# The last 128 rows of a matmul kernel in three column pieces (256, 128, 128) instead of two (256, 256)

## The chip, the cores and the metric

One core of one Trainium2 chip. The metric is the device time of one execution in microseconds; runs of one kernel mostly agree within 0.3%, and the trace of one profiled execution goes with each run. For the stretch that is changed I also use a finer measure, called the *tail*: from the start of the first matmul of the last 128 rows to the end of the span, both read from the trace. The tail leaves out the scatter of the 295 us ahead of it.

Some runs come out longer at a lower granted TensorE clock (0.983 to 0.987 here, where the others have 0.993 to 1.0). A run counts as slow when it is over 1.5% above the fastest of its kernel; ratios use the other runs, called fast.

## The reference

Attention over keys and values that are averaged in groups of 8, then a gated feed-forward layer. Only the last line matters here: the last matrix product.

```python
attn = softmax(scale * q @ pooled_k.T) @ pooled_v     # B=8, H=8, S=576, D=64
x = attn.transpose(0, 2, 1, 3).reshape(4608, 512)
h = x @ w_in                                          # 512 -> 2048
g = h * np.cos(h)
out = (g @ w_out).astype(np.float32)                  # 2048 -> 512
```

## The kernel before

Tokens are taken in 9 blocks of 512. For each, 2048 features are computed ("up", L297), gated (cos on ScalarE, product on VectorE), and multiplied back to 512 columns ("down", L310) in four chunks of 128 rows, `ms` = 0 to 3. Each chunk sums 16 matmuls in one PSUM bank. VectorE copies the bank to a buffer `o_sb` (L316), and two DMAs write 64 rows each to memory (L320). The very last chunk is done by `last_chunk`, which already cuts the 512 columns in two, so that the first half is copied and sent while the second is computed.

```python
msb = ctx.enter_context(tc.tile_pool(name="msb", bufs=3))     # o_sb, below, has 3 buffers
# ... (cut)
def down_out(t, ms, ps, c0=0, queues=(nc.sync, nc.sync)):
    o = msb.tile([128, d_model], FP32, name="o_sb", tag="o_sb")
    n = ps.shape[1]
    nc.vector.tensor_copy(out=o[:, 0:n], in_=ps)
    rows_of = out.rearrange("(b p t) m -> b t p m", b=B, t=ROW)
    for i, rows in enumerate(half):
        b_, pos = divmod((t * TILE + ms * 128) // 64 + i, ROW)
        queues[i].dma_start(out=rows_of[b_, ORDER[pos], :, c0:c0 + n], in_=o[rows, 0:n])

def last_chunk():
    t, ms = NT - 1, 3
    for hc in range(2):
        ps = banks[hc][:, 0, 0:256]
        for fc in range(FFCH):                                # FFCH = 16
            nc.tensor.matmul(ps, lhsT=g_sb[:, fc, ms * 128:(ms + 1) * 128],
                             rhs=w_out_sb[fc // 4][:, fc % 4, hc * 256:(hc + 1) * 256],
                             start=(fc == 0), stop=(fc == FFCH - 1))
        down_out(t, ms, ps, hc * 256, (nc.sync, nc.scalar))
# ... (cut)
        for n, (ms, fc) in enumerate(mms):                    # the other chunks
            # ... (cut)
            down_mm(obanks[ms % 2], ms, fc)
            if fc == FFCH - 1:
                down_out(t, ms, obanks[ms % 2])
    # ... (cut)
    last_chunk()
```

Every call of `down_out` takes the next of the three `o_sb` buffers, whatever the width of the piece. A copy into a buffer must wait until the two DMAs that last read that buffer have landed.

The softmax here doesn't subtract the row's maximum and nothing guards it: scores larger than these inputs give would overflow.

Of the kernel before, what the change touches and what calls it, by code (L numbers as in the profile page):

```python
# [19 lines left out]
def kernel(  # L20
# [9 lines left out]
    nc = tc.nc  # L30
# [31 lines left out]
    w_out_sb = [wpool.tile([128, 4, d_model], BF16, name=f"w_out_sb{i}") for i in range(4)]  # L62
# [9 lines left out]
    banks = [psum.tile([128, 2, 512], FP32, name=f"bank{i}") for i in range(3)]  # L72
# [240 lines left out]
# [9 lines that stand above are left out]
    def last_chunk():  # L322

        t, ms = NT - 1, 3
        for hc in range(2):
            ps = banks[hc][:, 0, 0:256]
            for fc in range(FFCH):
                nc.tensor.matmul(ps, lhsT=g_sb[:, fc, ms * 128:(ms + 1) * 128],  # L328
                                 rhs=w_out_sb[fc // 4][:, fc % 4, hc * 256:(hc + 1) * 256],
                                 start=(fc == 0), stop=(fc == FFCH - 1))  # L330
            down_out(t, ms, ps, hc * 256, (nc.sync, nc.scalar))


    EX = 5
# [90 lines left out]
    for t in range(NT):  # L425
# [69 lines left out]
        if b + 1 < B:  # L495
# [3 lines left out]
            pool_add(b + 1, "k")  # L499
            pool_add(b + 1, "v")  # L500
    last_chunk()
# [1 line left out]
_INS = ['q', 'k', 'v', 'moe_w_in', 'moe_w_out']  # L503
# [26 lines left out]
```

## Time and profile before

| | value | from |
|---|---|---|
| time | 305.36 us, median of 3 (304.97 to 305.43) | the runs |
| span of the profiled run | 303.0 us, clock 0.998 | the trace |
| first matmul of the last chunk | 295.56 us | timeline |
| end of its last matmul | 299.22 us | timeline: 295.56 + 3.66 |
| start and end of the last copy | 299.26, 299.68 us | timeline |
| last DMA issue, last landing | 299.71, 301.90 us | the trace's records of DMAs |
| tail | 302.96 - 295.56 = 7.40 us | the trace |

In the lines of the profile, PE is TensorE's matmuls, PEld its weight loads, DVE VectorE, ACT ScalarE and SP SyncE; a q, as in SPq, marks work of the engine's instruction queue, such as issuing a DMA. A DMA *lands* when its semaphore reports that its bytes are written. An entry such as L328 names the line of the kernel, `out<-in` the tiles, `x32` the count; a bracket holds the idle time before and what ended it. The durations of the copies, from the view of line L316 within the last 7 us (minimum / median / maximum in ns):

```profile
L316 DVE COPY o_sb<-bank x2: 425/426/426, 297.5 to 299.3; 128x256 f32<-128x256 f32 x2
L316 DVE COPY o_sb<-obank x1: 693/693/693, 295.8 to 295.8; 128x512 f32<-128x512 f32 x1
```

These two rows give the cost model of a copy that the prediction uses: 256 more columns cost 267 ns. The other lines that carry the argument stand in the prediction.

### The profile page before, as it was taken

To read this page: it belongs to the slowest core of one execution; us is meant where nothing else is said; L and a number is where in the kernel's file an instruction comes from. 1 tells how busy PE (TensorE), PEld (TensorE's weight loads), DVE (VectorE), ACT (ScalarE), POOL (GpSimd) and SP (SyncE) were. 2 spreads that over 40 slices of the span, in tenths; PEclk is the share of its full clock that TensorE was granted. 3 is DMA by queue.
4 is the path that set the end of the run, shared out by engine and by line. 5 is a ranking of instruction groups with operands and counts; after the bars stand their busy time and mean duration, and the time that the engine had idled before them with its cause. 6 is when DMAs were issued, how large, how long until landed. Compare 5 with 4: busy or idle time off the path is not lost.

```text
span 303.0 us, 4567 instructions
## 1 busy us (share of the span) xinstructions
PE 292.3 (96%) x1766; PEld 141.8 (47%) x1798; DVE 172.8 (57%) x211; ACT 206.8 (68%) x255; POOL 129.8 (43%) x92
## 2 busy tenths in 40 slices
PE   6899999999999999999999999999999999999995
PEld 2545544444544444444444544454444544444444
DVE  6458646564656465736575566656574657425712
ACT  3887896469866986698668876788569856605500
POOL 8553008975963893369534972399000000000000
PEclk9999999999999999999999999999999999999999
DMA  7999999739476935693369426952800330031032
GB/s 144 203 207 206 208 204 195 161 55 172 94 167 88 151 70 129 101 163 82 80 117 165 96 65 126 162 107 54 151 0 2 70 69 0 22 84 35 0 71 71
DMA packets 44006, 32.92 MB, mean 109 GB/s; under 512 B 22096, under 2 KB 39248, under 8 KB 43984
## 3 DMA queue, kind: packets, MB, share of 16 engines
q0 software_dynamic: 19744, 18.07, 38.4%
q1 hardware_dynamic: 24080, 14.42, 20.8%
q8 instruction: 14, 0.23, 0.3%
q10 hardware_dynamic: 160, 0.13, 0.2%
q14 instruction: 8, 0.07, 0.1%
HBM read 36.70 MB, written 9.44 MB: 152 GB/s over the span
## 4 chain that ended last, share of the span: by engine, by line
PE 88%; ACT 5%; issue 2%; DMA 2%; DVE 1%; DVEq 0%; ACTq 0%; POOLq 0%
PE bank L297 41%; PE obank L310 35%; PE bank L241 5%; PE bank L211 3%; DMA q_b<-in_q_dram 2%; ACT lnc L247 2%; ACT ex L218 1%; PE bank L328 1%; DVE xT L252 1%; ACT inv L248 1%; PE obank L157 0%; ACT L285 0%; PE obank L192 0%; ACT cos L304 0%; PE bank L165 0%
## 5 line engine op out<-in xcount | busy, mean ns | idle before, releaser
L310 PE MATMUL obank<-w_out_sb,g_sb 128*128 128x512 bf16 x542 | 130.5, 380 | 0.9
L297 PE MATMUL bank<-xT,w_in_sb 128*128 128x512 bf16 x563 | 125.7, 379 | 1.3
L304 ACT ACTIVATE cos<-bank,half_pi 128x1024 f32<-128x1024 f32 x72 | 80.0, 1113 | 62.2 <-PE bank L297 62.2
L307 DVE TENSOR_TENSOR g_sb<-bank,cos 128x1024 bf16<-128x1024 f32 x72 | 88.1, 1225 | 51.7 <-ACT cos L304 51.7
L297 PEld LDWEIGHTS <-w_in_sb 128*128 128x128 bf16 x576 | 56.1, 98 | 69.0 <-issue 2.8
L310 PEld LDWEIGHTS <-g_sb 128*128 128x128 bf16 x560 | 52.3, 98 | 57.0 <-issue 3.1
L252 DVE TENSOR_TENSOR xT<-bank,inv 64x512 bf16<-64x512 f32 (+1 forms) x72 | 45.3, 629 | 46.7 <-ACT inv L248 45.2
L141 POOL TENSOR_TENSOR kv_st<-kv_st 72x2048 f32<-72x2048 bf16 x12 | 48.7, 4062 | 35.0 <-DMA kv_st<-in_k_dram 35.0
L247 ACT ACTIVATE lnc<-bank 64x512 f32<-64x512 f32 (+1 forms) x72 | 39.2, 544 | 6.6 <-PE bank L241 5.6
L218 ACT ACTIVATE ex<-bank 72x1024 bf16<-72x1024 f32 (+1 forms) x40 | 35.5, 926 | 3.3 <-PE bank L211 3.2
L316 DVE COPY o_sb<-obank 128x512 f32<-128x512 f32 x35 | 24.2, 692 | 17.0 <-PE obank L310 13.4
L142 POOL TENSOR_TENSOR kv_st<-kv_st 72x1024 f32<-72x1024 f32 x12 | 28.2, 2348 | 1.0
L248 ACT ACTIVATE inv<-lnc 128x512 f32<-128x512 f32 (+1 forms) x36 | 21.0, 583 | 1.1
L241 PE MATMUL bank<-ex,vz 72*128 72x256 bf16 (+1 forms) x176 | 20.0, 243 | 0.2 <-ACT ex L218 0.2
L241 PEld LDWEIGHTS <-vz 72*128 72x128 bf16 x176 | 13.6, 97 | 10.2 <-DVE xT L252 1.7
L145 POOL TENSOR_TENSOR kp<-kv_st 72x512 bf16<-72x512 f32 x12 | 15.0, 1268 | 0.5
L211 PE MATMUL bank<-qT,kk 64*72 64x256 bf16 (+1 forms) x192 | 13.6, 252 | 0.9 <-ACT qT L193 0.5
L211 PEld LDWEIGHTS <-kk 64*72 64x72 bf16 x192 | 7.5, 109 | 11.1 <-issue 9.8
L285 ACT ACT_TABLE_LOAD x9 | 11.5, 1283 | 0.9 <-PEq L514 0.7
L288 ACT ACT_TABLE_LOAD x9 | 11.5, 1283 | 0.2
L494 POOL COPY gate<-kk 1x1 bf16<-1x1 bf16 x5 | 0.9, 179 | 24.1 <-DMA kk<-kp 24.1
L84 POOL DMA_DIRECT2D q_b<-in_q_dram x10 | 7.7, 772 | 2.8 <-DMA w_in_sb<-in_moe_w_in_dram 1.4
(55 smaller groups left out, 88.2 us busy)
## 6 DMA issues: line engine op xcount, KB each, us to landing
out_dram<-o_sb SPq DMA_DIRECT2D x70, 128.0 KB, 2.3
kv_st<-in_v_dram POOLq DMA_DIRECT2D x8, 576.0 KB, 13.3
kv_st<-in_k_dram POOLq DMA_DIRECT2D x7, 576.0 KB, 7.9
q_b<-in_q_dram POOLq DMA_DIRECT2D x6, 576.0 KB, 10.2
w_in_sb<-in_moe_w_in_dram POOLq DMA_DIRECT2D x4, 512.0 KB, 13.3
w_out_sb<-in_moe_w_out_dram POOLq DMA_DIRECT2D x4, 512.0 KB, 18.4
q_b<-in_q_dram POOLq DMA_DIRECT2D x4, 288.0 KB, 11.9
g_sb<-in_k_dram SPq DMA_DIRECT2D x1, 576.0 KB, 3.6
```

The lines of the kernel that those rows point to most:

```text
L141: add(out=s, in0=x[:, :, 0:4, :], in1=x[:, :, 4:8, :], op=ADD)
L142: add(out=s[:, :, 0:2, :], in0=s[:, :, 0:2, :], in1=s[:, :, 2:4, :], op=ADD)
L211: nc.tensor.matmul(pair[:Sp, bank, c:c + n].rearrange("p (g n) -> p g n", n=64), lhsT=kk[b % 2][half[r], h0 + i, 0:Sp], rhs=att["qT", b][h ...
L218: nc.scalar.activation(out=ex[:, 0:nh * n].rearrange("p (a n) -> p a n", a=2), in_=pair[:Sp, :, 0:nh * n // 2], func=ACTF.Exp, scale=scale ...
L241: nc.tensor.matmul(pair[:, hp, (i // 2) * n:(i // 2 + 1) * n], lhsT=vz[b % 2][:, pj, 2 * hp:2 * hp + 2, :].rearrange("p a d -> p (a d)"), ...
L247: nc.scalar.activation(out=lnc[half[1 - hp]], in_=pair[half[1 - hp], hp, 0:w], func=ACTF.Ln)
L252: nc.vector.tensor_mul(out=x_out(b, u, half[hp]), in0=cols(pair[half[hp], hp, :], u), in1=cols(inv[half[1 - hp]], u))
L297: nc.tensor.matmul(h[:, j, :], lhsT=w_in_sb[fc // 4][:, ki, (fc % 4) * 128:(fc % 4 + 1) * 128], rhs=xT[:, ki, t * TILE:(t + 1) * TILE], st ...
L304: nc.scalar.activation(out=cos, in_=h, func=ACTF.Sin, bias=half_pi[:, :1])
L307: nc.vector.tensor_mul(out=g_sb[:, 2 * fp:2 * fp + 2, :], in0=h, in1=cos)
L310: nc.tensor.matmul(o, lhsT=g_sb[:, fc, ms * 128:(ms + 1) * 128], rhs=w_out_sb[fc // 4][:, fc % 4, :], start=(fc == 0), stop=(fc == FFCH - 1))
L316: nc.vector.tensor_copy(out=o[:, 0:n], in_=ps)
```

## The change

A narrower last piece needs a shorter copy and a smaller transfer after the last matmul, when nothing else is left to overlap with. The price is 16 more matmuls, each with its own weight load.

```diff
     def last_chunk():
 
         t, ms = NT - 1, 3
-        for hc in range(2):
-            ps = banks[hc][:, 0, 0:256]
+        for i, (c0, n) in enumerate(((0, 256), (256, 128), (384, 128))):
+            ps = banks[i][:, 0, 0:n]
             for fc in range(FFCH):
                 nc.tensor.matmul(ps, lhsT=g_sb[:, fc, ms * 128:(ms + 1) * 128],
-                                 rhs=w_out_sb[fc // 4][:, fc % 4, hc * 256:(hc + 1) * 256],
+                                 rhs=w_out_sb[fc // 4][:, fc % 4, c0:c0 + n],
                                  start=(fc == 0), stop=(fc == FFCH - 1))
-            down_out(t, ms, ps, hc * 256, (nc.sync, nc.scalar))
+            down_out(t, ms, ps, c0, (nc.sync, nc.scalar))
```

## The prediction

> **What bounds the kernel now.** First the page: TensorE is busy for almost the whole span.
>
> ```profile
> span 303.0 us, 4567 instructions
> PE 292.3 (96%) x1766; PEld 141.8 (47%) x1798; DVE 172.8 (57%) x211; ACT 206.8 (68%) x255; POOL 129.8 (43%) x92
> ```
>
> The change is confined to the last 128 rows, so only the last 8 us can move. Next, the chain that ended last, in order of time, from 285 us on:
>
> ```profile
> 289.52 6.21 PE obank L310 x28
> 295.73 3.51 PE bank L328 x32
> 299.23 0.02 issue
> 299.26 0.42 DVE o_sb L316
> ```
>
> L328 is the changed loop, L316 the copy out of PSUM. The reader is to see matmuls without a gap, then one copy; nothing waits for an earlier engine. The timeline of the same stretch (start, duration, engine) gives the raw numbers:
>
> ```profile
> 295.35 3.59 PEld L328 LDWEIGHTS <-g_sb 128*128 128x128 bf16 x32
> 295.56 3.66 PE L328 MATMUL bank<-w_out_sb,g_sb 128*128 128x256 bf16 x32
> 297.51 0.43 DVE L316 COPY o_sb<-bank 128x256 f32<-128x256 f32 x1 [1.05 <-PE bank L328]
> 299.26 0.42 DVE L316 COPY o_sb<-bank 128x256 f32<-128x256 f32 x1 [1.32 <-PE bank L328]
> ```
>
> One matmul of 256 columns is recorded as 273 ns, so 32 of them step by (3.66 - 0.273) / 31 = 109 ns. The copy ends at 299.68. The rest of the span is shown by busy time per stretch (stretch, length, PE, PEld, DVE, ACT, POOL, clock, DMA share, GB/s):
>
> ```profile
> 299.90:300.80 0.90, 0.00 (x0) 0.00 (x0) 0.00 (x0) 0.00 (x0) 0.00 (x0) 1.00 0.00 0
> 300.80:301.60 0.80, 0.00 (x0) 0.00 (x0) 0.00 (x0) 0.00 (x0) 0.00 (x0) 0.96 0.64 164
> 301.60:303.00 1.40, 0.00 (x0) 0.00 (x0) 0.00 (x0) 0.00 (x0) 0.00 (x0) 0.50 0.00 0
> ```
>
> After the copy nothing moves for 0.9 us, bytes move for under 0.8 us, then comes about 1.1 us of closing semaphores and drains behind the last landing. The issues of that last piece (both start at 299.71) land after
>
> ```profile
> out_dram<-o_sb SPq DMA_DIRECT2D x1, 64.0 KB, 1.9
> out_dram<-o_sb ACTq DMA_DIRECT2D x1, 64.0 KB, 2.2
> ```
>
> so the last bytes are down at about 299.71 + 2.2 = 301.9. Of the 3.8 us from the last matmul's end (299.22) to the span's end, what depends on the piece's width is 0.42 us of copy and some of the 0.8 us of transfer. That is all that the change can attack.
>
> **What the Trainium skill says.** (1) "TensorE: Matmul & The Clock Gate", section "Back-to-back issue gap": a sustained stream of weight load and matmul at N=128 costs about 81 ns per matmul, an isolated stream N/2.4 + 2.5, about 56 ns. The trace has 128-column matmuls with new weights each time, the q transposes:
>
> ```profile
> 31.30 0.67 PE L192 MATMUL obank<-identity,q_b 128*128 128x128 bf16 x9
> ```
>
> Each is recorded as 219 ns, so they step by (0.67 - 0.219) / 8 = 56 ns: the trace sides with 56, and I use 57. The 256-column step of 109 ns agrees with N/2.4 + 2.5. (2) "VectorE: DVE Perf Modes", section "Why PSUM operands drop a tier": fp32 out of PSUM goes at one element per cycle, 0.96 GHz. The trace agrees: 693 ns at 512 columns, 426 at 256 (rows of L316), 1.04 ns per column, 159 ns fixed. (3) "DMA: Bandwidth & Descriptors", section "Anatomy of one DMA — SWDGE (gpsimd) path": about 2 us of a DMA are fixed, mostly the receipt of the last write. That is the other issuing path, but the trace agrees in kind: 128 KB land in 2.2 to 2.4 us, 64 KB in 1.9 to 2.2. (4) The same page's "Specifications": rows from 512 B up keep line rate. A 128-column float32 row is exactly 512 B; no output of this trace has that size.
>
> **The change part by part.** The second piece of 256 columns becomes two of 128.
>
> *TensorE.* Removed 16 x 109 = 1.744 us, added 32 x 57 = 1.824 us: +0.08 us. Starting at 295.56, the first piece takes 1.744, so B starts at 297.30 and C at 298.22; the last matmul starts at 298.22 + 15 x 0.057 = 299.07 and ends at 299.29 instead of 299.22. On the path: +0.07. B's end is 297.30 + 15 x 0.057 + 0.219 = 298.38.
>
> *Copies.* Each 128-column copy takes 159 + 128 x 1.04 = 292 ns. B's runs 298.41 to 298.70, under C's matmuls, free. C's is on the path in place of 426 ns: -0.13.
>
> *The output buffer.* Here is a new wait. o_sb has three buffers, and each piece takes one, so C takes that of the third-last write, the 512-column chunk copied at 295.76. The instruction order of the changed kernel, built but not run, confirms it: its last copy waits for exactly the two DMAs of that chunk. Before, the last copy waited for the chunk of 292.31, long landed. The second half of that chunk was issued at
>
> ```profile
> 297.00 0.65 SPq L320 DMA_DIRECT2D out_dram<-o_sb  x1
> ```
>
> and the DMA row for this issue alone says
>
> ```profile
> out_dram<-o_sb SPq DMA_DIRECT2D x1, 128.0 KB, 2.4
> ```
>
> hence landed at about 299.4. C's matmuls are done at 299.29, so the copy would be held about 0.11 us, and with two or three semaphore waits of the DVE's queue (36 ns median) it starts at about 299.48 instead of 299.33. Price: +0.15 on the path. C's copy then ends at 299.48 + 0.29 = 299.77, against 299.68: so up to the copy the change loses 0.09 us.
>
> *DMA.* B's two issues start at 298.73. SP is free (A's issue 297.97 + 0.47) and so is ACT (297.97 + 0.53). They end near 299.25, before C needs the queues, and B's bytes land near 300.8, just before C's start moving at about 299.80 + 1.1 = 300.9. C's two DMAs carry 32 KB each instead of 64. From 128 to 64 KB the landing on SP fell by 0.3 to 0.5 us, so halving again saves perhaps half as much, 0.15 to 0.25 (an estimate from these two sizes). Last landing: 299.80 + 2.2 - 0.2 = 301.8, against 301.9. The closing 1.1 us stays, with perhaps two more already satisfied semaphore waits of 28 ns: +0.03.
>
> Sum: TensorE +0.07, copy -0.13, buffer wait +0.15, DMA -0.2, close +0.03: about -0.1 us. On 305.36 us that is nothing: I predict 305.3 us.
>
> **The rivals.** *No buffer wait.* If the chunk lands 0.1 us earlier than I read, the gain is 0.25 us, 305.1. Against it stands the 2.4 us above, and the order of instructions. *Longer buffer wait.* Nothing new is queued ahead of that chunk's DMA, so it should not land later; if B's traffic delays it, +0.3 and 305.6. *Weight loads become the bound.* The PEld row records 98 ns per load; if 128-column matmuls stepped by that, 32 x (98 - 57) = +1.3 us, 306.6; at the skill's 81 ns +0.8 us, 306.1. The transposes speak against it, also 8 matmuls of 64 columns (L241) with full-width loads that took 0.39 us in all, about 28 ns a step. What is left of doubt is that transposes might be treated otherwise than accumulating matmuls. *DMA time is fixed.* If 32 KB land no sooner than 64 KB, or 512 B rows are slower, +0.1 us and 305.5.
>
> **Range and chances.** The three runs before span 0.46 us, more than any effect that I expect. The net effect lies between -0.4 (no wait, full DMA saving) and +0.4, rarely +1; with the scatter of a median that makes 304.7 to 305.9. Two per cent is 6.1 us, 1.6 times the whole tail after the last matmul: faster by 2% is impossible by this mechanism, slower by 2% needs a surprise such as another layout upsetting the body. Chances: faster 0.005, within 2% 0.985, slower 0.01.
>
> **What would show it.** Right: L328 has 16 matmuls of 256 and 32 of 128 columns stepping by 56 to 58 ns; the last copy is about 0.29 us; its start is released by an output DMA and not by L328, some 0.15 us after the last matmul's end; 32 KB issues land in 1.7 to 2.0 us; the span is within 0.3 us of 303.0. Wrong: a step of 80 or 98 ns; a last copy that starts 0.03 us after PE; landings still at 2.2 us; or a body before 295 us that differs.

## The result, and the profile after

The changed kernel took 304.9 us (median of 4 fast runs, 304.77 to 305.42); the kernel before, in the same rounds, 305.17 us (304.85 to 305.43). The ratio is 0.9995, with a 95% interval from 0.9978 to 1.0012: the same. Ratios in this text are the mean time of one kernel's fast runs over that of the other's fast runs of the same rounds, so they are not quite the ratio of the medians quoted.

The span is 303.1 us against 303.0, but the last chunk began 0.13 us later (295.69 against 295.56), for reasons outside the change: over the nine profiled fast runs, whose kernels differ only in the tail or in the number of output buffers, that start lay between 295.56 and 295.82. The tail is 303.08 - 295.69 = 7.39 us, against 7.40. So the change neither gained nor lost anything that can be seen, and the interest is in how that zero is made up.

The chain that ended last, from the changed kernel:

```profile
296.61 0.47 SPq L320
297.08 0.05 issue
297.13 2.37 DMA out_dram<-o_sb
299.50 0.03 issue
299.52 0.05 DVEq L316
299.57 0.04 issue
299.62 0.29 DVE o_sb L316
```

Before, TensorE led straight into the last copy. Now TensorE's work of the last chunk (L328) is not on the chain at all. The chain goes through the second DMA of the chunk `ms` = 2, issued at 297.13, whose landing at 299.50 frees the buffer that the third piece's copy writes; 0.12 us of semaphore handling later the copy starts. The timeline shows the same from VectorE's side:

```profile
295.69 3.70 PE L328 MATMUL bank<-w_out_sb,g_sb 128*128 128x256 bf16 x48
297.64 0.42 DVE L316 COPY o_sb<-bank 128x256 f32<-128x256 f32 x1 [1.05 <-PE bank L328]
298.53 0.29 DVE L316 COPY o_sb<-bank 128x128 f32<-128x128 f32 x1 [0.47 <-PE bank L328]
299.62 0.29 DVE L316 COPY o_sb<-bank 128x128 f32<-128x128 f32 x1 [0.79 <-DMA out_dram<-o_sb]
```

(The first row merges all three pieces and shows the shape of the first.) The last matmul ends at 295.69 + 3.70 = 299.39. The bracket of the last row is the one to read: the releaser is a DMA, and the copy starts 0.23 us after TensorE was done, where it was 0.04 before. The narrow matmuls, cut out of the timeline from 298.2 us on:

```profile
298.00 1.39 PE L328 MATMUL bank<-w_out_sb,g_sb 128*128 128x128 bf16 x22
```

With 219 ns for one, they step by (1.39 - 0.219) / 21 = 55.8 ns, and the whole chunk's matmuls take 3.70 us instead of 3.66. The landings of the last piece (issued at 299.94):

```profile
out_dram<-o_sb SPq DMA_DIRECT2D x1, 32.0 KB, 1.8
out_dram<-o_sb ACTq DMA_DIRECT2D x1, 32.0 KB, 2.0
```

against 1.9 and 2.2 for 64 KB. To two decimals, from the trace's own records of the ACT issue and its landing, 2.04 us against 2.19. And the busy time per stretch, the same stretches as in the prediction:

```profile
299.90:300.80 0.90, 0.00 (x0) 0.00 (x0) 0.01 (x1) 0.00 (x0) 0.00 (x0) 1.00 0.28 74
300.80:301.60 0.80, 0.00 (x0) 0.00 (x0) 0.00 (x0) 0.00 (x0) 0.00 (x0) 1.00 0.31 81
301.60:303.00 1.40, 0.00 (x0) 0.00 (x0) 0.00 (x0) 0.00 (x0) 0.00 (x0) 0.74 0.00 0
```

The second piece's bytes now fill the gap that was empty (share 0.28 where it was 0), and the third piece's need half the DMA time that the 256-column piece needed (0.31 against 0.64).

The terms of the tail, each as a difference to before:

| term | predicted | measured | how measured |
|---|---|---|---|
| end of the last matmul | +0.07 | +0.04 | 3.70 - 3.66 |
| wait between matmul and copy | +0.15 | +0.19 | 0.23 - 0.04 |
| last copy | -0.13 | -0.13 | 0.29 - 0.42 |
| issue to last landing | -0.2 | -0.15 | 2.04 - 2.19 |
| landing to end | +0.03 | +0.04 | 303.08 - 301.98, against 302.96 - 301.90 |
| sum | about -0.1 | -0.01 | tails: 7.39 - 7.40 |

### The profile page after: what moved, and what is told of

Same layout as the page of the kernel before. It is cut to its first block, busy times and chain, and to the rows that moved or that the text cites. A ratio compares the mean times of both kernels' runs of the same rounds, so it can differ in the third digit from the quotient of the medians.

```text
span 303.1 us, 4638 instructions
## 1 busy us (share of the span) xinstructions
PE 294.6 (97%) x1814; PEld 142.0 (47%) x1814; DVE 173.0 (57%) x212; ACT 206.8 (68%) x255; POOL 129.8 (43%) x92
## 4 chain that ended last, share of the span: by engine, by line
PE 80%; DMA 10%; ACT 3%; POOL 2%; issue 2%; DVE 1%; SPq 0%; DVEq 0%; ACTq 0%; POOLq 0%
PE bank L297 37%; PE obank L310 35%; DMA w_out_sb<-in_moe_w_out_dram 6%; PE bank L241 5%; DMA w_in_sb<-in_moe_w_in_dram 4%; PE bank L211 3%; ACT lnc L247 2%; DVE xT L252 1%; ACT inv L248 1%; DMA out_dram<-o_sb 1%; POOL kv_st L84 1%; POOL kp L384 1%; POOL q_b L84 1%; ACT L285 0%; ACT cos L304 0%
## 5 line engine op out<-in xcount | busy, mean ns | idle before, releaser
L310 PE MATMUL obank<-w_out_sb,g_sb 128*128 128x512 bf16 x560 | 132.5, 380 | 0.2 <-DMA w_out_sb<-in_moe_w_out_dram 0.2
```

Of the source, the lines that this page charges most:

```text
L310: nc.tensor.matmul(o, lhsT=g_sb[:, fc, ms * 128:(ms + 1) * 128], rhs=w_out_sb[fc // 4][:, fc % 4, :], start=(fc == 0), stop=(fc == FFCH - 1))
```

## The experiments

The theory: the narrower last piece does gain some 0.2 us, and the third output write gives it back, since it takes a buffer whose old content is still on its way to memory. The rivals: TensorE's longer work gives it back; or the transfers do, because their time hardly depends on size or because the pieces queue behind each other. All kernels gave correct results. Runs are compared with the kernel before in the same rounds; the first four ran together, the last four together, on another chip. Tails come from the one profiled execution of each.

The ratios of the first four need care. Two of the 11 runs of the kernel before in their rounds (308.43 and 308.6 us) had a clock of 0.983, and one of the changed kernel (308.38 us, experiment 4) had 0.987: the clock of slow runs, but they lie less than 1.5% above their fastest and count as fast. They widen the intervals, and the first two pull the ratios of experiments 1 to 3 down. Worked out again from the listed runs without these three, the ratios of experiments 1 to 4 are 0.9990, 1.0023, 0.9993 and 1.0001, without an interval.

### 1. Four output buffers

```diff
-        o = msb.tile([128, d_model], FP32, name="o_sb", tag="o_sb")
+        o = msb.tile([128, d_model], FP32, name="o_sb", tag="o_sb", bufs=4)
```

> The changed kernel with four output buffers instead of three; nothing else changes. The measure is the tail: from the start of the first matmul of the last 128 rows to the end of the span; 7.40 us before the change, 7.39 after. Theory (the last copy is held by its buffer, and this eats what narrower copy and transfer gain): the last copy starts 0.03 to 0.05 us after the last matmul's end, released by TensorE and not by a DMA, 0.19 us sooner than in the changed kernel; last landing and end move with it; tail 7.20. Rival 1 (the gain is eaten by the transfers: the 32 KB pieces queue behind each other, or their time is fixed): the copy moves by 0.19, the landing does not, tail 7.35 to 7.40. Rival 2 (TensorE's longer work is what eats it): tail unchanged, and the matmuls' part is over 3.75 us. Time 305.0 against 305.2 before, at the edge of what runs resolve.

Measured: tail 302.89 - 295.70 = 7.19 us; 304.68 us against 305.1 before, ratio 0.9967 (0.9923 to 1.0011). From the timeline:

```profile
295.70 3.70 PE L328 MATMUL bank<-w_out_sb,g_sb 128*128 128x256 bf16 x48
299.44 0.29 DVE L316 COPY o_sb<-bank 128x128 f32<-128x128 f32 x1 [0.60 <-PE bank L328]
```

TensorE's part is the same 3.70 us to the digit, the copy starts 0.04 us after it and is released by L328. Landing and end moved with it: the last landing came 2.06 us after its issue, and 2.04 in the changed kernel. So neither TensorE nor the transfers eat the gain; the buffer does, and it is worth 7.39 - 7.19 = 0.20 us. The time of whole runs leans the same way, but its interval holds 1, and most of the lean of 0.3% is that of the two low-clock runs: the tail resolves this, the time does not.

### 2. Two output buffers

```diff
-        o = msb.tile([128, d_model], FP32, name="o_sb", tag="o_sb")
+        o = msb.tile([128, d_model], FP32, name="o_sb", tag="o_sb", bufs=2)
```

> The changed kernel with two output buffers: the suspected wait is made larger. Theory: the second piece's copy now waits for the 512-column chunk (landed 3.80 us into the tail) and starts at 3.93 instead of 2.84; the third waits for the first piece's two DMAs (landed at 4.61) and starts at about 4.73 instead of 3.93, so the end comes 0.80 later: tail 8.2 and time 305.7 to 305.9. Rival (transfers or TensorE set the end, the buffer wait only takes slack): tail 7.4 to 7.6.

Measured: tail 304.05 - 295.79 = 8.26 us, time 305.65 us, ratio 1.0 (0.9951 to 1.0049; without the low-clock runs 1.0023). From the timeline:

```profile
297.74 0.42 DVE L316 COPY o_sb<-bank 128x256 f32<-128x256 f32 x1 [1.05 <-PE bank L328]
299.72 0.29 DVE L316 COPY o_sb<-bank 128x128 f32<-128x128 f32 x1 [1.56 <-DMA out_dram<-o_sb]
300.59 0.29 DVE L316 COPY o_sb<-bank 128x128 f32<-128x128 f32 x1 [0.58 <-DMA out_dram<-o_sb]
```

Now the second and the third copy both wait for a DMA, 3.93 and 4.80 us into the tail (expected 3.93 and 4.73). With two, three and four buffers the tail is 8.26, 7.39 and 7.19: the wait can be made larger and smaller at will, and the end follows.

### 3. Pieces of 384 and 128 columns

```diff
-        for i, (c0, n) in enumerate(((0, 256), (256, 128), (384, 128))):
+        for i, (c0, n) in enumerate(((0, 384), (384, 128))):
```

> Two pieces of 384 and 128 columns, three buffers as before: the narrow last piece without the third piece, so that the last copy takes the buffer of a chunk long landed. Theory: matmuls 16 x 162.5 + 15 x 56 + 219 ns = 3.66 us, copy from 3.70 to 3.99, no DMA wait, issues at 4.02, the last landing 2.04 later and 1.1 to close: tail 7.16. The rival for this one: the first piece's 192 KB are still on the DMA queues when the last piece's bytes start (about 4.5 to 5.6 against 5.14), so that the last landing comes 0.1 to 0.3 us later: tail 7.25 to 7.45.

Measured: tail 302.82 - 295.61 = 7.21 us (expected 7.16); 304.75 us (median of 5 fast runs; the sixth, 309.56 us, was slow), ratio 0.9971 (0.9922 to 1.0019). From the timeline, and from the DMAs of its last piece:

```profile
295.61 3.66 PE L328 MATMUL bank<-w_out_sb,g_sb 128*128 128x384 bf16 x32
298.41 0.56 DVE L316 COPY o_sb<-bank 128x384 f32<-128x384 f32 x1 [1.91 <-PE bank L328]
299.30 0.29 DVE L316 COPY o_sb<-bank 128x128 f32<-128x128 f32 x1 [0.34 <-PE bank L328]
```

```profile
out_dram<-o_sb SPq DMA_DIRECT2D x1, 32.0 KB, 2.0
out_dram<-o_sb ACTq DMA_DIRECT2D x1, 32.0 KB, 2.1
```

With only two writes there is no DMA wait even with three buffers, and the copy ends 3.98 us into the tail (expected 3.99). The last landing, that of the ACT half, came late: it was issued at 299.65, 0.03 us after the SP half, and took 2.13 us instead of 2.04. The SP half took 2.0 instead of 1.8, but it is not the last. The first piece's ACT half landed only at 301.43, so the two pieces were under way at once, as the rival says; that this costs the 0.09 us is likely and not shown, and the whole stays below the rival's 7.25. This form reaches the same end as four buffers without using one.

### 4. The changed kernel again, beside these

> The changed kernel unchanged, in the same rounds as the experiments, to compare with: tail 7.39 within 0.05, last copy released by an output DMA again, time within 0.2 us of the kernel before.

Measured: tail 303.00 - 295.63 = 7.37 us, last copy again 0.23 us after TensorE and released by a DMA; 305.17 us (median of 5 fast runs; the sixth, 309.68 us, was slow), ratio 1.0 (0.9942 to 1.0059). The tail repeats within 0.02 us; the run times of these rounds scatter because of the low-clock runs named above.

### 5. The kernel before with two output buffers

```diff
-        o = msb.tile([128, d_model], FP32, name="o_sb", tag="o_sb")
+        o = msb.tile([128, d_model], FP32, name="o_sb", tag="o_sb", bufs=2)
-        for i, (c0, n) in enumerate(((0, 256), (256, 128), (384, 128))):
+        for i, (c0, n) in enumerate(((0, 256), (256, 256))):
```

(The minus lines are those of the changed kernel, from which the file was made; pieces of 256 and 256 are the kernel before.)

> The kernel before (two pieces of 256) with two output buffers. If the wait comes from counting writes back through the buffers, the second piece now takes the buffer of the 512-column chunk that held the changed kernel's third piece: landed 3.80 to 3.86 us into the tail, so the last copy starts at about 3.98 instead of 3.70, released by a DMA, and the tail is 7.68 instead of 7.40. Rival (the wait belongs to the third piece, by its DMAs on busy queues, and not to the buffer): the copy follows the last matmul by 0.04 and the tail stays 7.40.

Measured: tail 303.46 - 295.82 = 7.64 us (expected 7.68); 305.45 us, ratio 1.0009 (0.999 to 1.0028).

```profile
295.82 3.66 PE L328 MATMUL bank<-w_out_sb,g_sb 128*128 128x256 bf16 x32
299.76 0.42 DVE L316 COPY o_sb<-bank 128x256 f32<-128x256 f32 x1 [1.56 <-DMA out_dram<-o_sb]
```

The old kernel shows the new kernel's wait once it has one buffer less: the copy starts 3.94 us into the tail, the time at which the changed kernel's third copy starts (299.62 - 295.69 = 3.93). The wait belongs to counting writes back through the buffers, not to the third piece.

### 6. One piece of 512 columns

```diff
-        for i, (c0, n) in enumerate(((0, 256), (256, 128), (384, 128))):
+        for i, (c0, n) in enumerate(((0, 512),)):
```

> The last 128 rows in one piece of 512 columns: what the whole splitting buys. Matmuls 15 x 215.7 + 379 ns = 3.61 us, copy 0.69 from 3.65, issues at 4.37, 256 KB from about 5.5; at the rate of the chunk before (128 packets of 2 KB in 1.45 us) to 6.95, landing 7.3, 1.07 to close: tail 8.35, time about 306.1 against 305.1. If transfer time did not depend on size, the tail would be 4.37 + 2.2 + 1.07 = 7.65.

Measured: tail 303.72 - 295.57 = 8.15 us; 305.63 us, ratio 1.0016 (0.9994 to 1.0039). The landings of the last issue, at 299.95:

```profile
out_dram<-o_sb SPq DMA_DIRECT2D x1, 128.0 KB, 2.3
out_dram<-o_sb ACTq DMA_DIRECT2D x1, 128.0 KB, 2.6
```

Copy and matmuls came as expected (issue 4.38 us into the tail); I had the landing 0.3 us too late; the close took 1.18 us instead of 1.07. In the trace's records of DMA packets, the 128 packets of 2 KB started within 1.03 us here, on two queues, and within 1.30 us for the 512-column chunk ahead of it, two DMAs in a row on SP's queue; that the second queue makes the difference is likely, not tested. Cutting in two had bought 8.15 - 7.40 = 0.75 us; the second cut was worth 0.2 at best (experiments 1 and 3).

### 7. Pieces of 256, 192 and 64 columns, four buffers

```diff
-        o = msb.tile([128, d_model], FP32, name="o_sb", tag="o_sb")
+        o = msb.tile([128, d_model], FP32, name="o_sb", tag="o_sb", bufs=4)
-        for i, (c0, n) in enumerate(((0, 256), (256, 128), (384, 128))):
+        for i, (c0, n) in enumerate(((0, 256), (256, 192), (448, 64))):
```

> Pieces of 256, 192 and 64 columns with four buffers: the split taken further, rows of 256 bytes in the last. Matmuls 16 x 109 + 16 x 82.5 + 15 x 28 + 192 ns = 3.68; last copy 226 ns, from 3.72 to 3.94, no DMA wait. But the second piece's issues start at 3.66 and take 0.47 (SP) and 0.5 to 0.63 (ACT), so the last issue on ACT starts at 4.2 to 4.3; landing 1.95 later, 1.07 to close: tail 7.25, no better than the 7.19 of 256, 128, 128 with four buffers. If the issues do not get in each other's way: 7.0 to 7.05. If rows of 256 bytes are slow: landing 2.1 us or more after the issue, tail 7.4.

Measured: tail 303.07 - 295.72 = 7.35 us; 305.01 us, ratio 0.9994 (0.9978 to 1.0009). From the chain, the last copy; from the timeline of SP, the second piece's issue; and the landings of the last piece:

```profile
299.45 0.23 DVE o_sb L316
```

```profile
299.37 0.47 SPq L320 DMA_DIRECT2D out_dram<-o_sb  x1
299.93 0.55 SPq L320 DMA_DIRECT2D out_dram<-o_sb  x1
```

```profile
out_dram<-o_sb SPq DMA_DIRECT2D x1, 16.0 KB, 1.8
out_dram<-o_sb ACTq DMA_DIRECT2D x1, 16.0 KB, 2.0
```

The last copy ends at 299.68, but its DMA is issued at 299.93, only after the second piece's issue is through (299.84): 0.25 us from copy to issue, where the changed kernel needs 0.03 (read from the trace, not tested by a run). And half the bytes land hardly sooner: 2.02 us on ACT after 2.04. The last ACT issue came 4.26 us into the tail, as expected (4.2 to 4.3); the expected 7.25 was 0.1 too low, 0.07 of it because the landing had been put at 1.95. The direction holds: going further made the tail 0.16 us longer than the 7.19 of four buffers with 256, 128, 128.

### 8. Four output buffers, again

> The changed kernel with four output buffers a second time, for a narrower interval and as the neighbour of the finer split: tail 7.19 within 0.05, time 0.2 us (0.07%) below the kernel before, which the interval may or may not resolve.

Five of six runs were fast; the median of all six is 305.02 us, the ratio of the fast ones 0.9993 (0.9975 to 1.0011). The profiled execution fell in the slow state (clock 0.983, 309.98 us), so I do not use its span; its tail, 308.20 - 301.00 = 7.20 us, stands as an aside, since the last chunk ran as in experiment 1. The time is not resolved in either set of rounds: a gain of 0.2 us is 0.07%, under the width of both intervals. What is shown for four buffers, and for 384 and 128, is a tail shorter by 0.2 us than that of both kernels; that the program as a whole is faster is not shown.

## Why the prediction was right

It said 305.3 us and no visible change; 304.9 us and a ratio of 0.9995 came out. The difference of 0.4 us between forecast and median is not the tail's: the tail moved 0.01 us, and the kernel before had itself moved from 305.36 to 305.17 when runs were added. The number alone supports no mechanism: three of the rivals (305.1, 305.5 and 305.6 us) lie in the same range. The terms of the tail tell them apart.

By its own steps. *TensorE, +0.07*: right in kind. The step is 55.8 ns, so neither the 98 ns of a recorded weight load nor the skill's 81 ns bounds this stream, and the transposes were a good stand-in; +0.04 came, because the step of 57 had been rounded up from 56. The tail did not feel the difference, since the last copy waits for a landing and not for TensorE. *Copy, -0.13*: exact, 292 ns predicted and measured. *The output buffer, +0.15*: the wait exists, is released by the DMA named, and cost 0.19; experiments 1, 2 and 5 turn it off, enlarge it and carry it over to the old kernel. It is longer by about what TensorE was sooner: the copy started 3.93 us into the tail, predicted 299.48 - 295.56 = 3.92. In that a little luck: the chunk landed 0.05 us sooner in the tail, and from landing to copy 0.12 us passed instead of the 0.08 predicted. The step was read from two things that stand in no stall row of the old profile: the number of writes back to the same buffer, and the issue time plus 2.4 us of landing. *DMA, -0.2*: mis-sized, -0.15. The estimate continued a slope from 128 to 64 KB; with experiments 6 and 7 the last landing is 2.59, 2.19, 2.04 and 2.02 us for 128, 64, 32 and 16 KB each. The saving per halving falls away (0.40, 0.15, 0.02), and about 2 us are fixed. *Close, +0.03*: +0.04 measured; over the runs cut in two or three it was 1.04 to 1.10 us, and no run shows what sets it.

Of its rivals, "weight loads become the bound" fell by the 55.8 ns, and "no buffer wait" by the chain. That rival had named 305.1 us and a gain of 0.25; experiment 1, which removes the wait, gained 0.20 of the tail, so its size was about right too. "DMA time is fixed" fell for this change (2.04 us for 32 KB after 2.19 for 64), but holds from there to 16 KB. "B's traffic delays the chunk" did not happen: its landing took 2.37 us, and 2.41 before.

## What to carry to other kernels

When the work at a kernel's end is cut finer, count how many buffers back each new piece reaches, and compare that with how long a write needs to land (2.4 us here): with three buffers, a narrower last piece that lies three writes behind a large one waits for it if its matmuls end before that write has landed. Choose the cut so that the last piece is narrow and the number of pieces small (384 and 128 did as well here as three pieces with another buffer), and stop where the previous piece's DMA issue (0.47 to 0.64 us for the middle pieces here) is not yet through. And measure a change of tenths of a microsecond by the stretch that it changes, not by the time of the whole program.

## What the Trainium skill lacked or had wrong

- "TensorE: Matmul & The Clock Gate", "Back-to-back issue gap", gives about 81 ns per matmul at N=128 and 131 ns at N=512 for a sustained stream of weight loads and matmuls. Here, with a new 128x128 weight load for each, the steps were 55.8 ns at 128 columns (the changed kernel), 109 at 256 (before) and (3.62 - 0.379) / 15 = 216 at 512 (experiment 6). The formula N/2.4 + 2.5, which the section gives for the isolated case, fits all three.
- "VectorE: DVE Perf Modes", "The TRN2 errata — SBUF-src ops pay a fixed extra latency per instruction", gives 120 cycles plus one per fp32 column for a copy out of PSUM, 258 ns for 128 columns by its formula; the runs show 292 ns there and 424 to 426 at 256, a fixed part of about 159 ns.
- "DMA: Bandwidth & Descriptors", "Anatomy of one DMA — SWDGE (gpsimd) path", fits a fixed 2 us for the path of GpSimd. The stores from SP and ACT agree: issued together, the later one landed after 2.59, 2.19, 2.04 and 2.02 us for 128, 64, 32 and 16 KB each. But the ACT half landed 0.26 to 0.33 us after the SP half (0.17 in the last piece of experiment 3), which neither this section nor the one on issuing engines mentions.
- The same page's "Issuing engines are not separate DMA queues" calls the sequencer's time for an issue usually small beside the DMA itself. Here, in the tails, it was 0.47 to 0.74 us on SP and 0.50 to 0.78 on ACT, against landings of 1.8 to 2.6 us, and in experiment 7 the last issue came 0.25 us after its copy, once the issue before it was through.
- The same page's "Specifications" puts a limit for line rate at 512 B. With 64 rows per DMA, rows of 256 B showed no penalty in landing (2.02 us for 16 KB against 2.04 for 32 KB in rows of 512 B); at this size the fixed part may hide one.
